# Masked scores stay in PSUM through exponential, copy and low pass

## The chip, the cores and the metric

The kernel runs on one core of a Trainium2 chip. The metric is the time of one execution on the device, in microseconds (us). Five engines work beside each other and are ordered by semaphores only: TensorE (PE in the profile; its weight loads are PEld), VectorE (DVE), ScalarE (ACT), GpSimd (POOL) and SyncE (SP), which issues most DMAs.

## The reference

Two layers in a row, in float32. First causal attention with a learned decay, for 8 batches of 8 heads, 576 positions and head size 64; then a two-layer network with a hard-swish product on the 4608 tokens.

```
scores = q @ k.T / 8
cum    = cumsum(log(clip(f, 1e-4, 1)))
scores = where(causal, -1e9, scores + cum[:, None] - cum[None, :])
attn   = exp(scores - max(scores)); attn = attn / (sum(attn) + 1e-9)
x      = (attn @ v), heads side by side      # 4608 x 512
h      = x @ w_in                            # 4608 x 2048
out    = (h * clip(h + 3, 0, 6) / 6) @ w_out # 4608 x 512
```

## The kernel before, in words

Precision is kept by splitting: a float32 operand becomes a high and a low float16 part, and a product takes three matmuls (high by high, high by low, low by high). The second part is made by a "low pass", x minus its high part.

The first batch is computed in another way (kinds A and B, lines 565 to 596), within the first 140 us or so, while the weights are loaded and split. The other 56 heads are of kind F and go through `rows` (line 621); this is what the change touches. A head is done in two halves, given by `NAT = ((1, 4, 0), (2, 3))`: each number c is a block of up to 128 query rows, with RB[c] + RR[c] keys before and in it (192, 576, 64 and 320, 448). For each half:

- L636 and L639: TensorE writes the scores of the blocks to one PSUM buffer `pn` of 1024 columns, which is two banks of 512. `PLACE` gives the column at which each block starts. The pool `ps_s` has two such buffers, so in effect one for each half.
- L647: VectorE adds the causal mask W, scales, and takes each row's extreme into `mc`. Its result goes to `pp`, a float32 tile in SBUF (832 columns, two buffers).
- L656: ScalarE takes the exponential, from `pp` to `pp`, with the row's extreme as bias.
- L673: ScalarE copies `pp`, scaled, as float16 into the tile `hl` (a `ring` buffer): the high part.
- L619, the helper `low`: VectorE computes the low part from `pp` and the high part, into `hl`. A head has seven of these: 128x128 and 128x512, then one over two strips of 64 columns and one of 64x64 in the first half; 128x256, 128x384 and again the two strips in the second. The view `pair` takes the two strips from `at[a]` and `at[b]` and needs them in rising order.
- L694: a DMA transposes `hl` into `pT`, from which the products with V are computed (L719 to L724).

Beside this, the network's tiles (`moe_tile`: L808 to L810, L816 to L821, then L863 to L873) are issued in small units between the steps of a head by a credit count. GpSimd prepares the split Q and K of the coming heads (L463 to L476). A planner at build time sets the order on each engine from the order of issue, the dependencies and its own estimates of durations; on the chip each engine goes through its list in order.

`decay` (line 173) reads the decay factors f at the start, takes their logarithm and the running sum. Its tiles fs and lf use the same SBUF buffers as `pp` (tag Pp). `xT` is the transposed input of the network's tiles, two buffers, and is written by DMA from L775 on.

Of the kernel before, what the change touches and what calls it, by code (L numbers as in the profile page):

```python
# [11 lines left out]
F32 = mybir.dt.float32  # L12
# [8 lines left out]
def kernel(  # L21
# [12 lines left out]
    NHEAD, D, S = qk.shape  # L34
# [5 lines left out]
    P = 128  # L40
# [14 lines left out]
    p2 = ctx.enter_context(tc.tile_pool(name="p2", bufs=2))  # L55
# [32 lines left out]
    W = cpool.tile([P, 4 * P + P], BF16, name="W")  # L88
# [59 lines left out]
    xT = [cpool.tile([P, NCC, TT // P, 2, P], F16, name=f"xT{i}") for i in range(2)]  # L148
# [24 lines left out]
    def decay():  # L173
        warm = p2.tile([1, 1], F32, tag="m1", name="warm")
        nc.vector.memset(warm, 1.0)
        nc.scalar.activation(warm, warm, AF.Ln)
        fs = p2.tile([NHEAD, S], F32, tag="Pp", name="fs")
        nc.sync.dma_start(fs, f)
        yield
        zf = p2.tile([NHEAD, S], F32, tag="PHL", name="zf")  # L180
        nc.vector.memset(zf, 0.0)
        nc.vector.tensor_scalar(fs, fs, 1e-4, 1.0, op0=ALU.max, op1=ALU.min)
        lf = p2.tile([NHEAD, S], F32, tag="Pp", name="lf")
        nc.scalar.activation(lf, fs, AF.Ln)
        nc.scalar.activation(warm, lf[0:1, 0:1], AF.Exp)
        cum = p2.tile([NHEAD, S], F32, tag="xf", name="cum", bufs=1)
        nc.vector.tensor_tensor_scan(cum[:, :], lf, zf, 0.0, op0=ALU.add, op1=ALU.add)
        nc.vector.tensor_scalar(cs[:, 0, :], cum, 8.0, None, op0=ALU.mult)
        d = nc.vector.scalar_tensor_tensor(
            cs[:, 1, :], cum, 8.0, cs[:, 0, :].bitcast(F32), op0=ALU.mult, op1=ALU.subtract  # L190
        )
        decayed.append(d.ins)
        yield
# [415 lines left out]
    o = 0  # L609
    for half in NAT:  # L610
        for c in half:
            HT[c] = o
            o += (2 * c + 1) * P
    PLACE = {1: 0, 4: 192, 0: 768, 3: 0, 2: 512}
    ringh = [t.bitcast(F16) for t in ring]
    clean = set()

    def low(out_, x, hi):
        nc.vector.scalar_tensor_tensor(out_, x, PSC, hi, op0=ALU.mult, op1=ALU.subtract)  # L619

    def rows(v):
        i, j = v % NQK, v % NL
        n = VH[v][1]
        pT = p2.tile([P, 3200], F16, tag="PHL", name=f"pT_{v}")
        mc = MF[v % 2]
        e0 = 0
        for half in range(2):
            pn = ps_s.tile([P, 1024], F32, tag="S", name=f"pn_{v}_{half}")
            hl = ringh[(2 * v + half) % NRING]
            for c in NAT[half]:  # L630
                o, r, kw = PLACE[c], RR[c], RB[c] + RR[c]
                cut = [0] + [x for x in (512 - o, ) if 0 < x < kw] + [kw]
                qs = slice(RB[c], RB[c] + r)
                for a, e in zip(cut, cut[1:]):
                    dst = pn[:r, o + a:o + e]
                    nc.tensor.matmul(  # L636
                        dst, TQ[i][0:D + 4, qs], TK[i][0:D + 4, a:e], start=True, stop=False
                    )
                    nc.tensor.matmul(  # L639
                        dst, T7[j][:, qs], T1[j][:, a:e], start=False, stop=True  # L640
                    )
            pp = p2.tile([P, 832], F32, tag="Pp", name=f"pp_{v}_{half}")
            at, w = {}, 0
            for x, c in enumerate(NAT[half]):
                o, r, kw = PLACE[c], RR[c], RB[c] + RR[c]
                at[c] = w
                nc.vector.tensor_tensor_reduce(  # L647
                    pp[:r, w:w + kw], pn[:r, o:o + kw], W[:r, 4 * P + r - kw:4 * P + r],
                    -0.125, 3.0e38, ALU.add, ALU.min, accum_out=mc[:r, e0 + x:e0 + x + 1],
                )  # L650
                w += kw
            e1 = e0 + len(NAT[half])
            for x, c in enumerate(NAT[half]):
                r, kw = RR[c], RB[c] + RR[c]
                x_ = pp[:r, at[c]:at[c] + kw]
                nc.scalar.activation(  # L656
                    x_, x_, AF.Exp, bias=mc[:r, e0 + x:e0 + x + 1], scale=-1.0
                )
            e0 = e1
            yield  # L660

            def pair(t, a, b):
                return t[:, a:a + 2 * (b - a)].rearrange("p (n w) -> p n w", n=2)[:, :, 0:64]

            h0 = {c: GH[half][c] + c * P + 64 for c in NAT[half]}
            slot = (2 * v + half) % NRING
            if 0 in NAT[half] and slot not in clean:
                nc.gpsimd.memset(hl[64:, h0[0] - 64:h0[0] + 64], 0.0)
                if w_out_done:
                    clean.add(slot)  # L670
            for c in NAT[half]:
                r, kw, a = RR[c], RB[c] + RR[c], GH[half][c]
                nc.scalar.activation(  # L673
                    hl[:r, h0[c]:h0[c] + kw], pp[:r, at[c]:at[c] + kw], AF.Copy, scale=PSC
                )
                if c:
                    low(
                        hl[:r, a:a + c * P], pp[:r, at[c] + 64:at[c] + kw],
                        hl[:r, h0[c] + 64:h0[c] + kw],
                    )  # L680
            a, b = NAT[half][:2]
            low(
                pair(hl, h0[a] - 64, h0[b] - 64), pair(pp, at[a], at[b]),
                pair(hl, h0[a], h0[b]),
            )
            if 0 in NAT[half]:
                low(
                    hl[:64, h0[0] - 64:h0[0]], pp[:64, at[0]:at[0] + 64],
                    hl[:64, h0[0]:h0[0] + 64],
                )  # L690

            w = sum((2 * c + 1) * P for c in NAT[half])
            d = HT[NAT[half][0]]
            nc.sync.dma_start_transpose(  # L694
                pT[:, d:d + w].rearrange("p (g t) -> p g t", t=P), hl[:, 0:w]
            )
            yield pT
# [213 lines left out]


    dec = decay()
    w_in_q = w_in_work()
    w_out_q = w_out_work()
# [93 lines left out]
    for i, (kind, n) in enumerate(VH):  # L1009
# [13 lines left out]
        if moved is not None:  # L1023
            done(moved)
            moved = None
        rates[0] = F_RATE[0] if kind == "B" else F_RATE[b] if b < 2 else even(h)
        sg = rows(i) if kind == "F" else scores(i)
        front = ahead and VH[i + 2][0] != "F"
        next(sg)
# [93 lines left out]
```

## Time and profile before

| | |
|---|---|
| median of 3 runs | 1063.89 us (1061.79 to 1065.01) |
| the profiled execution | 1063.62 us, span in the trace 1061.8 us |
| mean granted TensorE clock | 0.977 |
| TensorE busy | 1023.8 us, 96% |
| VectorE busy | 779.1 us, 73% |
| ScalarE busy | 600.5 us, 57% |
| GpSimd busy | 422.2 us, 40% |

The shares are means over the whole span. The profile divides it: where an engine is busy all the time and where it waits differs by stage, and a line of code stands in the profile as L and its number in the listing.

### The profile page before, as it was taken

What the parts mean: (1) busy time and instruction counts of PE and PEld (TensorE: products, weight loads), DVE (VectorE), ACT (ScalarE), POOL (GpSimd) and SP (SyncE); (2) the same over time, 40 slices, a digit from 0 to 9 for tenths busy, and PEclk for the clock granted to TensorE, in tenths of its full rate; (3) what the DMA queues carried; (4) which work ended last, traced back from release to release, by engine and by line L of the source; (5) the groups of instructions that cost most, each with busy time, mean ns of one, the idle gap of its engine ahead of it and who ended that gap; (6) DMA issues with size and microseconds to landing.
All of it is one profiled execution on the core that took longest, in us unless ns stands there. A gap on an engine that the chain in (4) does not pass through costs nothing.

```text
span 1061.8 us, 20746 instructions
## 1 busy us (share of the span) xinstructions
PE 1023.8 (96%) x7833; PEld 616.2 (58%) x7833; DVE 779.1 (73%) x1927; ACT 600.5 (57%) x1190; POOL 422.2 (40%) x430
## 2 busy tenths in 40 slices
PE   6789999889999999999999999999999999999998
PEld 4567867655555755555555755555555755545545
DVE  8788998999986679876976679876976788505500
ACT  4678676776664557655654556655754577405500
POOL 7455774565452444444334244444424442000000
PEclk8699999889999999999999999999999999999999
DMA  8665325778555555466443474456444534410000
GB/s 301 212 193 161 92 59 125 148 139 169 115 94 101 117 142 104 80 131 149 83 88 89 101 157 97 97 127 143 82 94 84 103 80 78 81 30 11 1 20 30
DMA packets 248415, 114.34 MB, mean 108 GB/s; under 512 B 224788, under 2 KB 226124, under 8 KB 248316
## 3 DMA queue, kind: packets, MB, share of 16 engines
q1 hardware_dynamic: 248284, 113.03, 46.9%
q8 instruction: 61, 1.00, 0.4%
q14 instruction: 38, 0.31, 0.1%
q10 hardware_dynamic: 32, 0.01, 0.0%
HBM read 47.93 MB, written 9.73 MB: 54 GB/s over the span
## 4 chain that ended last, share of the span: by engine, by line
PE 66%; DVE 19%; DMA 6%; ACT 4%; issue 3%; SPq 1%; DVEq 0%; ACTq 0%
PE po L863 11%; PE po L865 11%; PE po L864 11%; PE ph L808 6%; PE ph L810 6%; PE ph L809 6%; DVE ring L619 6%; DMA vst<-in_vS_dram 3%; PE pn L639 3%; PE pn L636 3%; DVE pp L647 2%; DVE gT L821 2%; DVE r L819 2%; DVE vm L382 1%; DVE w L311 1%
## 5 line engine op out<-in xcount | busy, mean ns | idle before, releaser
L619 DVE SCALAR_TENSOR_TENSOR ring<-pp,ring 128x128 f16<-128x128 f32 x392 | 237.4, 645 | 51.1 <-ACT ring L673 49.0
L463 POOL TENSOR_SCALAR TK<-ST 64x576 fp32r<-64x576 f32 (+1 forms) x68 | 57.2, 841 | 430.2 <-PE pn L636 395.0
L863 PE MATMUL po<-w,gT 128*128 128x512 f16 x560 | 210.1, 382 | 0.0
L864 PE MATMUL po<-w,gT 128*128 128x512 f16 x560 | 209.2, 381 | 0.5 <-DVE w L311 0.3
L865 PE MATMUL po<-w,gT 128*128 128x512 f16 x560 | 209.1, 381 | 0.0
L808 PE MATMUL ph<-xT,w 128*128 128x512 f16 (+1 forms) x576 | 201.7, 359 | 6.2 <-DVE r L819 6.2
L809 PE MATMUL ph<-xT,w 128*128 128x512 f16 (+1 forms) x576 | 201.0, 358 | 0.0
L810 PE MATMUL ph<-xT,w 128*128 128x512 f16 (+1 forms) x576 | 200.9, 358 | 0.0
L656 ACT ACTIVATE pp<-pp,MF 128x192 f32<-128x192 f32 x280 | 147.7, 554 | 89.8 <-DVE MF L647 88.7
L647 DVE CUSTOM_DVE_ANT_0 pp<-pn,W 128x192 f32<-128x192 f32 x280 | 123.3, 480 | 20.2 <-PE pn L639 19.9
L636 PE MATMUL pn<-TK,TQ 68*128 68x192 f32 x336 | 125.3, 386 | 3.4 <-DVE MF L647 3.0
L820 ACT CAST gT<-r 128x512 f16<-128x512 f32 (+1 forms) x144 | 81.4, 567 | 76.7 <-DVE r L819 75.8
L816 ACT ACTIVATE r<-ph,bias_r,SC 128x512 f32<-128x512 f32 (+1 forms) x144 | 103.2, 721 | 35.6 <-PE ph L810 23.7
L673 ACT ACTIVATE ring<-pp 128x192 f16<-128x192 f32 x280 | 119.6, 458 | 1.5
L821 DVE TENSOR_TENSOR gT<-r,gT 128x512 f16<-128x512 f32 (+1 forms) x144 | 101.2, 706 | 23.9 <-ACT gT L820 22.4
L819 DVE SCALAR_TENSOR_TENSOR r<-r,ph 128x512 f32<-128x512 f32 (+1 forms) x144 | 88.7, 618 | 40.0 <-ACT r L816 40.0
L639 PE MATMUL pn<-T,T 128*128 128x192 f32 x336 | 115.4, 369 | 0.0
L476 POOL TENSOR_TENSOR T<-ST,T 64x576 fp32r<-64x576 f32 (+1 forms) x68 | 108.3, 1593 | 5.1
L473 POOL TENSOR_TENSOR T<-ST,TQ 64x576 fp32r<-64x576 f32 (+2 forms) x68 | 96.4, 1417 | 5.4
L873 ACT ACTIVATE o<-po,SC 128x512 f32<-128x512 f32 (+1 forms) x37 | 24.8, 669 | 123.6 <-PE po L865 122.2
L865 PEld LDWEIGHTS <-gT 128*128 128x128 f16 x560 | 54.7, 98 | 68.3 <-issue 8.8
L864 PEld LDWEIGHTS <-gT 128*128 128x128 f16 x560 | 54.8, 98 | 59.8 <-issue 5.4
(150 smaller groups left out, 2010.6 us busy)
## 6 DMA issues: line engine op xcount, KB each, us to landing
ST<-in_qk_dram SPq DMA_DIRECT2D x64, 288.0 KB
out_dram<-o SPq DMA_DIRECT2D x33, 256.0 KB
ring<-in_w_out_dram SPq DMA_DIRECT2D x16, 512.0 KB
vst<-in_vS_dram SPq DMA_DIRECT2D x7, 1040.0 KB
ring<-in_w_in_dram SPq DMA_DIRECT2D x9, 512.0 KB
w<-in_w_in_dram SPq DMA_DIRECT2D x7, 512.0 KB
vst<-in_vS_dram SPq DMA_DIRECT2D x14, 130.0 KB
pT<-ring SPq DMA_TRANSPOSE x112
```

The costliest lines, as they stand in the source:

```text
L619: nc.vector.scalar_tensor_tensor(out_, x, PSC, hi, op0=ALU.mult, op1=ALU.subtract)
L636: nc.tensor.matmul(dst, TQ[i][0:D + 4, qs], TK[i][0:D + 4, a:e], start=True, stop=False)
L639: nc.tensor.matmul(dst, T7[j][:, qs], T1[j][:, a:e], start=False, stop=True)
L647: nc.vector.tensor_tensor_reduce(pp[:r, w:w + kw], pn[:r, o:o + kw], W[:r, 4 * P + r - kw:4 * P + r], -0.125, 3.0e38, ALU.add, ALU.min, ac ...
L656: nc.scalar.activation(x_, x_, AF.Exp, bias=mc[:r, e0 + x:e0 + x + 1], scale=-1.0)
L808: nc.tensor.matmul(ph, w1[0][:, cc, fs_], xh, start=(cc == 0), stop=False)
L809: nc.tensor.matmul(ph, w1[0][:, cc, fs_], xl, start=False, stop=False)
L810: d = nc.tensor.matmul(ph, w1[1][:, cc, fs_], xh, start=False, stop=(cc == NCC - 1))
L821: nc.vector.tensor_tensor(gT[:, 1, fc, c0:c1], r, gT[:, 0, fc, c0:c1], op=ALU.subtract)
L863: nc.tensor.matmul(po, g[:, 0, fc, ts_], w2[:, fc, 0, c], start=(fc == 0), stop=False)
L864: nc.tensor.matmul(po, g[:, 0, fc, ts_], w2[:, fc, 1, c], start=False, stop=False)
L865: d = nc.tensor.matmul(po, g[:, 1, fc, ts_], w2[:, fc, 0, c], start=False, stop=(fc == NFC - 1))
```

## The change

`pp` is no longer a tile of its own: the masked scores go back to where they were read, in the PSUM buffer `pn`; the exponential is taken there, and the copy and the low pass read from there. `PLACE` exchanges the places of c = 2 and c = 3, so that `pair` finds the two strips in rising order. fs and lf, which used the buffers of `pp`, lie in the first `xT` buffer.

```
-        fs = p2.tile([NHEAD, S], F32, tag="Pp", name="fs")
+        fs = xT[0].bitcast(F32).rearrange("p a c l t -> p (a c l t)")[0:NHEAD, 0:S]
...
-        lf = p2.tile([NHEAD, S], F32, tag="Pp", name="lf")
+        lf = xT[0].bitcast(F32).rearrange("p a c l t -> p (a c l t)")[0:NHEAD, S:2 * S]
...
-    PLACE = {1: 0, 4: 192, 0: 768, 3: 0, 2: 512}
+    PLACE = {1: 0, 4: 192, 0: 768, 2: 0, 3: 512}
...
-            pp = p2.tile([P, 832], F32, tag="Pp", name=f"pp_{v}_{half}")
-            at, w = {}, 0
+            pp, at = pn, PLACE
             for x, c in enumerate(NAT[half]):
                 o, r, kw = PLACE[c], RR[c], RB[c] + RR[c]
-                at[c] = w
                 nc.vector.tensor_tensor_reduce(
-                    pp[:r, w:w + kw], pn[:r, o:o + kw], W[:r, 4 * P + r - kw:4 * P + r],
+                    pn[:r, o:o + kw], pn[:r, o:o + kw], W[:r, 4 * P + r - kw:4 * P + r],
                     -0.125, 3.0e38, ALU.add, ALU.min, accum_out=mc[:r, e0 + x:e0 + x + 1],
                 )
-                w += kw
```

## Rows read from the trace of the kernel before

**Rows 1.** The page's busy time of TensorE, us, share of the span, instructions.

```profile
PE 1023.8 (96%) x7833; PEld 616.2 (58%) x7833; DVE 779.1 (73%) x1927; ACT 600.5 (57%) x1190; POOL 422.2 (40%) x430
```

**Rows 2.** Windows: length, busy PE, PEld, DVE, ACT, POOL; granted clock, DMA.

```profile
140.00:200.00 60.00, 53.86 (x459) 37.97 (x458) 55.08 (x155) 40.15 (x89) 33.06 (x29) 0.98 0.59 123
200.00:300.00 100.00, 95.92 (x794) 58.56 (x795) 95.27 (x247) 68.76 (x146) 54.24 (x51) 0.94 0.68 135
300.00:400.00 100.00, 100.00 (x875) 60.44 (x873) 70.67 (x181) 52.70 (x108) 42.66 (x42) 1.00 0.55 115
...
930.00:1000.00 70.00, 70.00 (x464) 37.38 (x462) 22.75 (x33) 26.42 (x40) 0.00 (x0) 1.00 0.04 13
```

**Rows 3.** Waits of TensorE, 140 to 300 us: us in total, times, longest.

```profile
PE pav L719 <- DMA pT<-ring: 4.3, 3, 1.7
PE pn L636 <- DVE MF L647: 3.0, 1, 3.0
PE ph L808 <- DVE r L819: 2.0, 2, 1.2
```

**Rows 4.** Waits of TensorE, 300 to 930 us (all of them).

```profile
PE ph L808 <- DVE r L819: 2.2, 6, 0.7
```

**Rows 5.** The page's costliest groups: count, busy us, mean ns, idle before.

```profile
L619 DVE SCALAR_TENSOR_TENSOR ring<-pp,ring 128x128 f16<-128x128 f32 x392 | 237.4, 645 | 51.1 <-ACT ring L673 49.0
...
L647 DVE CUSTOM_DVE_ANT_0 pp<-pn,W 128x192 f32<-128x192 f32 x280 | 123.3, 480 | 20.2 <-PE pn L639 19.9
```

**Rows 6.** Groups by line and form, 896 to 930 us.

```profile
L619 DVE SCALAR_TENSOR_TENSOR ring<-pp,ring 128x128 f16<-128x128 f32 x6 | 1.7, 283 | 0.1
...
L619 DVE SCALAR_TENSOR_TENSOR ring<-pp,ring 128x512 f16<-128x512 f32 x2 | 1.4, 690 | 1.2 <-ACT ring L673 1.2
...
L619 DVE SCALAR_TENSOR_TENSOR ring<-pp,ring 128x384 f16<-128x384 f32 x2 | 1.1, 548 | 0.0
...
L619 DVE SCALAR_TENSOR_TENSOR ring<-pp,ring 128x256 f16<-128x256 f32 x2 | 0.8, 414 | 0.0
...
L619 DVE SCALAR_TENSOR_TENSOR ring<-pp,ring 64x64 f16<-64x64 f32 x2 | 0.4, 212 | 0.0
```

**Rows 7.** Timeline, 208 to 226 us: start us, duration us, what, [idle before].

```profile
208.99 0.39 PE L636 MATMUL pn<-TK,TQ 68*128 68x320 f32 x1
...
214.09 3.19 DVE L619 SCALAR_TENSOR_TENSOR ring<-pp,ring 128x256 f16<-128x256 f32 x3
...
215.19 1.47 POOL L476 TENSOR_TENSOR T<-ST,T 64x576 fp32r<-64x576 f32 x1
...
218.22 0.61 DVE L647 CUSTOM_DVE_ANT_0 pp<-pn,W 128x448 f32<-128x448 f32 x1
...
218.89 0.64 PE L636 MATMUL pn<-TK,TQ 68*128 68x320 f32 x1 [2.99 <-DVE MF L647]
...
223.26 2.10 DVE L619 SCALAR_TENSOR_TENSOR ring<-pp,ring 128x384 f16<-128x384 f32 x2
```

**Rows 8.** Line 819's instructions: durations in ns, least, median, most.

```profile
L819 DVE SCALAR_TENSOR_TENSOR r<-r,ph x144: 373/674/690, 98.3 to 1006.6; 128x512 f32<-128x512 f32 x112, 128x256 f32<-128x256 f32 x32
```

**Rows 9.** Groups of VectorE by line, 150 to 250 us, the costliest.

```profile
L619 DVE SCALAR_TENSOR_TENSOR ring<-pp,ring 128x128 f16<-128x128 f32 (+4 forms) x67 | 38.8, 619 | 0.1
```

**Rows 10.** Groups by line and form, whole span: ScalarE's exponentials of 576 columns.

```profile
L656 ACT ACTIVATE pp<-pp,MF 128x576 f32<-128x576 f32 x56 | 42.7, 762 | 2.5 <-DVE MF L647 2.4
...
L593 ACT ACTIVATE pf<-ps,bias_p 128x576 f32<-128x576 f32 x8 | 5.9, 736 | 0.0
```

**Rows 11.** Line 775's transposing DMAs into x: durations, first and last start.

```profile
L775 SPq DMA_TRANSPOSE xT<-xhl x36: 1190/1233/3077, 58.6 to 927.7; - x36
```

**Rows 12.** Timeline, 320 to 337 us: scores and the last lows of one half.

```profile
320.87 0.44 PE L636 MATMUL pn<-TK,TQ 68*128 68x192 f32 x1
...
326.81 1.02 DVE L619 SCALAR_TENSOR_TENSOR ring<-pp,ring 128x512 f16<-128x512 f32 x3 [1.19 <-ACT ring L673]
...
336.90 0.44 PE L636 MATMUL pn<-TK,TQ 68*128 68x192 f32 x1
```

## The prediction

> **What bounds the kernel now.** I read the busy table first: TensorE is busy 96% of the span [rows 1]. A busy figure this high says little about how near an engine is to its peak, so the next view is busy time by stretch [rows 2]. In it the reader should see three stages. From 300 us on TensorE has no gap at the full granted clock (1.00) while VectorE has 29 us of slack in a hundred; in the last stage GpSimd is idle and VectorE busy for a third. Nothing that VectorE saves there can shorten anything. From 140 to 300 us it is otherwise: TensorE is idle for 60.00 - 53.86 = 6.1 us and 100.00 - 95.92 = 4.1 us, together 10.2 us, while VectorE is busy for 55.08 of 60 and 95.27 of 100 us. That stage alone is bound by VectorE. It also shows granted clocks of 0.98 and 0.94, which is 0.02 x 60 + 0.06 x 100 = 7.2 us of full-speed clock not given, next to the idle time.
>
> The view of waits says who was late there [rows 3]. The largest wait is for a transposed P: that DMA starts when the last low pass of its half is written. The next is for the masks of a scores buffer, the third for the eviction of an MoE tile. All end on VectorE or on a DMA that VectorE released. After 300 us the same view has 2.2 us in all [rows 4]. So the most that a lighter VectorE can give back is 10.2 + 7.2 + 2.2 = 19.6 us, a little less since clock lost in idle time is counted twice. Everything before 140 us stays as it is: the change touches nothing there except two buffers.
>
> **The change: the low pass.** The low pass (L619) is the costliest VectorE group, and the edit to it is the one that carries the gain. Its rows look wrong for their size: 392 instructions at a mean of 645 ns [rows 5], although the window in which GpSimd has no work left shows the same forms at 690, 548, 414, 283 and 212 ns [rows 6]. A head has one each of the first three, three of 128x128 and one of 64x64: 690 + 548 + 414 + 3 x 283 + 212 = 2713 ns. The 392 are 56 heads, so undisturbed they would take 56 x 2.71 = 152 us, and they take 392 x 0.645 = 253 us. Some 101 us are lost beside GpSimd. The timeline shows it happening: three lows that should take 0.41 + 0.55 + 0.28 us take 3.19 us from 214.09 on, beside a GpSimd subtraction that starts at 215.19; the masks of the same stretch come behind them and end at 218.83, and TensorE, idle for 2.99 us, starts its scores at 218.89 [rows 7].
>
> What would an instruction of this kind take with one input in PSUM and one in SBUF? The MoE product (L819) is the same operation with exactly that pair of inputs: over 144 instructions in all stages its maximum is 690 ns for a median of 674 [rows 8], so it is never stretched, and 128x512 costs what the undisturbed low pass costs [rows 6]. I take the low pass after the change at its undisturbed figures. That is 101 us less on VectorE over the kernel. In the stretch that matters, 150 to 250 us, it is 67 x 619 = 41.5 us [rows 9] against 67/7 x 2.71 = 26.0 us, so 15.5 us less. Bounds: nothing, if the stretching had another cause; 15.5 us, if all goes.
>
> The Trainium skill says otherwise on one point: "Perfetto Trace Analysis", section "Optimizing Scalar/DVE Operations", gives VectorE about 60 ns of access overhead on SBUF and 125 ns on PSUM. Its 65 ns on 67 lows would leave about 11 us of the 15.5, and, with half of 19.6 x 11/15.5, a forecast some 3 us later than mine. The rows show no such difference at 128x512 (at most 690 ns with an input in PSUM, 690 without), so the sum goes by them.
>
> **The masks and ScalarE.** The mask pass (L647, 123.3 us in 280 instructions, [rows 5]) now writes PSUM where it reads. No row of before shows VectorE reading and writing one bank. From below it costs nothing (same count, same columns); from above, if a read and a write in one bank halved its rate, it doubles: 123 us more, which would eat the low pass's 101 us. I take nothing, because the low pass and the MoE product move the same columns at the same rate whether or not an operand is in PSUM. The exponentials now read and write PSUM: the one exponential that reads PSUM takes 736 ns at 576 columns, the SBUF one 762 [rows 10]. So ScalarE gains up to 26 ns on each of 560 instructions, 15 us, or nothing. It is not the bound in any row of [rows 2]; I count zero, and what would uncover it is ScalarE being held by VectorE (second rival).
>
> **Buffers at nothing.** fs and lf go into the first x buffer. They are read in the opening of the kernel and the first transposed x lands only from 58.6 us on [rows 11], so no wait arises; instruction counts are the same. The new PLACE changes banks, not the number or order of matmuls.
>
> **The wait that is added.** A scores buffer is now held from its first matmul to its last low pass; before, to its last mask. There are two, one for each half. In the later stage this is covered: scores begin at 320.87, the last low ends at 326.81 + 1.02 = 327.83, the next scores for that buffer begin at 336.90 [rows 12]. The hold is 7.0 us and 9.1 us are to spare. Between 150 and 250 us it is not: scores that begin at 208.99 have their last low at 223.26 + 2.10 = 225.36, a hold of 16.4 us, and the next ones began at 218.89, 6.5 us before that [rows 7]. Left in the same order TensorE would wait these 6.5 us instead of 2.99. Behind the waiting scores stand MoE and P.V matmuls, since TensorE goes in order; whoever evicts those waits in turn. Against it stand the lows: of the 16.4 us, 3.19 - 1.24 = 1.95 us are stretch in the lows ahead of its masks and about 1.3 us more (2.10 against 0.548 + 0.283) in its last ones. And the order is not fixed: the planner that sets it sees the longer hold, and can put MoE matmuls ahead of the scores.
>
> **Sum.** The reachable 19.6 us are reduced by the new hold. With VectorE down from 96 in a hundred toward 80 in the stretch, its backlog should go, and with it the three waits of [rows 3]; the hold keeps some. Between all and nothing I take half: 9.8 us. The profiled execution took 1063.62 us (span 1061.8 and 1.8 around it), which lies 0.3 us under the median of the runs, 1063.89. So 1063.6 - 9.8 = 1053.8, say 1054 us. The later 900 us stay as they are.
>
> **Rivals.**
> No gain: the idle time between 140 and 300 us belongs to the order and to transposes, not to VectorE's speed, or the in-place masks eat what the lows give. For it: the largest wait of [rows 3] names a DMA. Against it: that DMA follows a low pass. Time: 1060.4 to 1066.8, most likely the old 1063.6.
>
> Slower, by the hold: between 150 and 250 us, 67/7 = 9.6 heads pass, one in 10.4 us [rows 9]. A hold over 10.4 us cannot keep this pace with one buffer for each half, and that is the point from which it decides. Midway between the two holds seen (7.0 and 16.4) is 11.7 us: 9.6 x (11.7 - 10.4) = 12.5 us, all on TensorE, nothing regained: 1076 us. For it: the 16.4 us. Against it: VectorE's lighter load, and MoE matmuls to put between.
>
> Slower, by shared banks: the copy (ScalarE) and the low pass (VectorE) now read the same bank. If two engines cannot be in one bank at a time, then in the half with c = 1, 4, 0, whose c = 4 lies across both banks, copy and low must alternate: the copy of c = 4 waits for the low of c = 1 (0.28 us), that of c = 0 for the low of c = 4 (0.69 us), about 1.0 us of held ScalarE in every head. Behind it on ScalarE stand the evictions of the MoE tiles, for which TensorE waits. Over the 46 heads outside the stretch that is 46 us if nothing hides it; the 2.2 us of [rows 4] say that eviction has slack, so a third, 15 us, which with the gain kept gives 1069 us. The Trainium skill states the rule behind it: "PSUM — Partial Sum Buffer", section "PSUM bank collisions raise a hardware error", says that two engines in one bank and quadrant collide, reads included, and have to be ordered. No row of before shows the two engines in one bank.
>
> **How the numbers follow.** Forecast (1043 to 1060): 0.57. No gain: 0.20. Hold: 0.14. Banks: 0.09. Faster by over 0.3% (3.2 us, about what the three runs can tell from no change) is the first, 0.57; within 0.3% the second, 0.20; slower the last two, 0.23. The low end is the reachable sum, 1063.6 - 19.6 = 1044, less 1 us for the spread of the runs. The high end takes in the banks' 1069 and the lighter part of the hold, 1072; above it lies some 0.08.
>
> **What would show it.** Right: L619 at 2.7 us for a head with no stretched instruction; VectorE's busy time down by some 85 to 100 us; TensorE's idle time from 140 to 300 us below 6 us at a clock of 0.97 or more; nothing changed after 930 us but its start. Wrong: scores matmuls (L636) that wait for the low pass by more than 10 us in total, which is the hold; ScalarE's copies (L673, now with almost no idle time before them) waiting for lows by 40 us or more together with longer MoE waits, which is the banks; L647 well over 480 ns in the mean, which is the in-place mask. If all three are absent and the time is still 1064, the idle time was the order's.

## The result and the profile after

The changed kernel takes 1076.03 us (1075.33 to 1077.67), before 1063.89: a ratio of 1.0119, 95% interval 1.0099 to 1.0138. It is slower by 1.2%; the forecast was 1054 us, a gain. The profiled execution after took 1077.67 us, span 1075.9. Line numbers fall by two to three: masks L647 is now L645, exponentials L656 L653, copies L673 L670, V products L719 L716, the network's L808 to L810 and L863 to L865 now L805 to L807 and L860 to L862.

The busy table of after answers to [rows 1]. VectorE and GpSimd are lighter, TensorE is busy for longer.

```profile
PE 1029.8 (96%) x7833; PEld 625.7 (58%) x7833; DVE 699.6 (65%) x1927; ACT 586.3 (54%) x1190; POOL 395.5 (37%) x430
```

The costliest groups of after, for those of [rows 5], with the exponentials and the copies beside them (busy us, mean ns, idle before and what ended it):

```profile
L653 ACT ACTIVATE pn<-pn,MF 128x192 f32<-128x192 f32 (+1 forms) x280 | 132.8, 496 | 132.1 <-DVE MF L645 110.1
...
L645 DVE CUSTOM_DVE_ANT_0 pn<-pn,W 128x192 f32<-128x192 f32 x280 | 134.8, 501 | 75.6 <-PE pn L639 72.7
L619 DVE SCALAR_TENSOR_TENSOR ring<-pn,ring 128x128 f16<-128x128 f32 (+1 forms) x392 | 137.0, 386 | 58.1 <-ACT ring L670 56.7
L670 ACT ACTIVATE ring<-pn 128x192 f16<-128x192 f32 (+1 forms) x280 | 114.2, 433 | 39.6 <-DVE ring L619 36.5
```

The low pass did what was forecast: 386 ns in the mean against 645, 100 us less. The in-place mask pays 21 ns. New is the 36.5 us in which ScalarE's copies wait for lows. VectorE's busy time falls by 79.5 us, from 779.1 to 699.6. So no operation became dear enough to explain the loss, which must lie in waits. Two windows of after, for those of [rows 2] (length, busy PE, PEld, DVE, ACT, POOL, granted clock, DMA share, GB/s):

```profile
200.00:300.00 100.00, 85.83 (x710) 54.66 (x707) 70.86 (x223) 59.34 (x132) 45.15 (x48) 0.88 0.57 118
...
930.00:1000.00 70.00, 70.00 (x482) 36.64 (x482) 21.42 (x41) 24.26 (x40) 0.00 (x0) 1.00 0.14 35
```

VectorE is no longer full between 200 and 300 us (70.86 against 95.27), and yet TensorE is idle there for 14.2 us instead of 4.1, at a clock of 0.88 instead of 0.94. Cut at other places, the same view separates two stretches. First after:

```profile
140.00:230.00 90.00, 84.02 (x701) 57.96 (x700) 68.14 (x213) 53.59 (x121) 34.62 (x36) 0.98 0.47 101
230.00:280.00 50.00, 35.83 (x286) 24.09 (x284) 33.06 (x103) 25.60 (x57) 23.41 (x27) 0.76 0.64 130
...
330.00:930.00 600.00, 597.39 (x4778) 345.93 (x4776) 407.11 (x1142) 340.03 (x691) 227.01 (x238) 1.00 0.52 107
```

and before:

```profile
140.00:230.00 90.00, 80.61 (x703) 57.64 (x703) 83.89 (x235) 60.74 (x137) 52.08 (x47) 0.92 0.61 126
230.00:280.00 50.00, 49.16 (x420) 28.42 (x419) 48.31 (x126) 33.27 (x67) 26.44 (x24) 1.00 0.79 162
...
330.00:930.00 600.00, 597.80 (x4804) 343.12 (x4803) 460.20 (x1125) 346.73 (x683) 232.59 (x229) 1.00 0.49 105
```

Up to 230 us TensorE does better after the change: 3.4 us less idle time, and 0.06 x 90 = 5.4 us of clock more. From 230 to 280 us it loses 49.16 - 35.83 = 13.3 us and 0.24 x 50 = 12 us of clock (the two overlap, since a clock that is low in idle time costs nothing). From 330 to 930 us the difference is 0.4 us. So the loss shows in one stretch of 50 us.

What TensorE did up to 230 us shows why. In groups by line of 140 to 230 us, before, and the masks of that stretch (five to a head):

```profile
L863 PE MATMUL po<-w,gT 128*128 128x512 f16 x41 | 16.4, 405 | 0.0
...
L647 DVE CUSTOM_DVE_ANT_0 pp<-pn,W x39: 207/477/753, 139.9 to 227.8; 128x576 f32<-128x576 f32 x8, 64x64 f32<-64x64 f32 x8, 128x320 f32<-128x320 f32 x8, 128x448 f32<-128x448 f32 x8
```

The same two groups after:

```profile
L860 PE MATMUL po<-w,gT 128*128 128x512 f16 x61 | 23.2, 380 | 0.8 <-DVE r L816 0.8
...
L645 DVE CUSTOM_DVE_ANT_0 pn<-pn,W x30: 215/500/767, 140.7 to 225.3; 128x192 f32<-128x192 f32 x6, 128x576 f32<-128x576 f32 x6, 128x320 f32<-128x320 f32 x6, 64x64 f32<-64x64 f32 x6
```

The network's line L860 has issued 61 matmuls instead of 41 (L861 and L862 likewise), and six heads are masked instead of eight. The planner, which sees the longer hold, filled TensorE with the network's first tile. That looks like a gain, and is work taken from later: from 230 to 280 us the same group has 4 matmuls where there were 23 before. What is then left is the chain of heads, and the timeline of after shows its pace (start us, duration us, what, [idle before]; rows of three engines, put together):

```profile
234.66 0.44 PE L636 MATMUL pn<-TK,TQ 68*128 68x192 f32 x1
235.90 0.37 DVE L645 CUSTOM_DVE_ANT_0 pn<-pn,W 128x192 f32<-128x192 f32 x1 [4.76 <-PE pn L639]
237.68 0.66 DVE L645 CUSTOM_DVE_ANT_0 pn<-pn,W 128x448 f32<-128x448 f32 x1
237.92 1.74 ACT L653 ACTIVATE pn<-pn,MF 128x192 f32<-128x192 f32 x4 [4.77 <-DVE MF L645]
...
242.99 2.10 DVE L619 SCALAR_TENSOR_TENSOR ring<-pn,ring 128x256 f16<-128x256 f32 x6
243.44 0.81 ACT L670 ACTIVATE ring<-pn 128x448 f16<-128x448 f32 x2 [1.07 <-DVE ring L619]
...
239.02 0.19 PE L721 MATMUL pav<-v,pT 128*128 128x65 f16 x1
244.87 0.50 PE L636 MATMUL pn<-TK,TQ 68*128 68x192 f32 x1 [5.67 <-ACT ring L670]
...
253.56 0.33 PE L636 MATMUL pn<-TK,TQ 68*128 68x192 f32 x1 [0.87 <-ACT v L413]
260.21 0.24 PE L716 MATMUL pav<-v,pT 128*128 128x65 f16 x1 [4.76 <-DMA pT<-ring]
...
263.00 0.50 PE L636 MATMUL pn<-TK,TQ 68*128 68x192 f32 x1 [0.44 <-issue]
270.93 0.62 PE L805 MATMUL ph<-xT,w 128*128 128x512 f16 x1
```

The engines take turns: masks to 238.3, exponentials from 237.9, copies and lows to 245.1. The next scores start at 244.87, behind the copies and lows that read their buffer (the row x6 holds the lows of both halves; the view names a copy); before, the buffer would have been free with the masks. From 239.2 to 244.87 TensorE has nothing it may do. The heads follow 10.2, 8.7 and 9.4 us apart. Only the first of these starts ends a wait for the buffer; ahead of the last, TensorE waited 4.76 us for a transposed P. The two largest waits of TensorE from 140 to 300 us (total, times, longest), for [rows 3]:

```profile
PE pav L716 <- DMA pT<-ring: 8.5, 3, 4.8
PE pn L636 <- ACT ring L670: 5.7, 1, 5.7
```

The largest is again a transposed P, which follows the last low; the second is the hold itself. Other waits on L636 add only 1.3 us.

What TensorE lacks in the gap is x. One DMA moves the x of a pair of heads, and the network's tile of a batch needs four pairs. Here are the second and the fourth of the second batch, before:

```profile
212.52 1.99 SPq L775 DMA_TRANSPOSE xT<-xhl  x1
...
252.89 1.34 SPq L775 DMA_TRANSPOSE xT<-xhl  x1
```

and after:

```profile
223.20 1.42 SPq L772 DMA_TRANSPOSE xT<-xhl  x1
...
266.43 1.72 SPq L772 DMA_TRANSPOSE xT<-xhl  x1
```

The fourth starts 13.5 us later, and the span is longer by 14.1 us. Of that delay 10.7 us are there at the second pair already, in the stretch in which TensorE looks better. Before, TensorE begins the network's second tile at 253.6 us. After, it begins it at 232.3 with the x that is there, nine matmuls of each line, and goes on at 270.93, behind the fourth pair:

```profile
L805 PE MATMUL ph<-xT,w x9: 379/379/650, 232.3 to 250.6; 128*128 128x512 f16 x9
```

### The profile page after: what moved, and what is told of

Same layout as the page of the kernel before. It is cut to its first block, busy times and chain, and to the rows that moved or that the text cites. A ratio compares the mean times of both kernels' runs of the same rounds, so it can differ in the third digit from the quotient of the medians.

```text
span 1075.9 us, 20862 instructions
## 1 busy us (share of the span) xinstructions
PE 1029.8 (96%) x7833; PEld 625.7 (58%) x7833; DVE 699.6 (65%) x1927; ACT 586.3 (54%) x1190; POOL 395.5 (37%) x430
## 4 chain that ended last, share of the span: by engine, by line
PE 82%; DVE 8%; DMA 5%; ACT 2%; issue 1%; SPq 1%; DVEq 0%; ACTq 0%
PE po L860 11%; PE po L862 11%; PE po L861 11%; PE ph L805 10%; PE ph L806 10%; PE ph L807 9%; PE pn L636 4%; PE pn L639 4%; DMA pT<-ring 2%; PE pav L720 2%; PE pav L721 2%; PE pav L719 1%; PE pav L727 1%; DMA ring<-in_w_in_dram 1%; DMA vst<-in_vS_dram 1%
## 5 line engine op out<-in xcount | busy, mean ns | idle before, releaser
L463 POOL TENSOR_SCALAR TK<-ST 64x576 fp32r<-64x576 f32 (+1 forms) x68 | 50.6, 744 | 473.2 <-PE pn L636 433.1
L860 PE MATMUL po<-w,gT 128*128 128x512 f16 x560 | 208.7, 380 | 0.8 <-DVE r L816 0.8
L861 PE MATMUL po<-w,gT 128*128 128x512 f16 x560 | 208.3, 379 | 0.0
L862 PE MATMUL po<-w,gT 128*128 128x512 f16 x560 | 208.1, 379 | 0.0
L805 PE MATMUL ph<-xT,w 128*128 128x512 f16 (+1 forms) x576 | 202.1, 360 | 5.7 <-DVE r L816 5.7
L653 ACT ACTIVATE pn<-pn,MF 128x192 f32<-128x192 f32 (+1 forms) x280 | 132.8, 496 | 132.1 <-DVE MF L645 110.1
L807 PE MATMUL ph<-xT,w 128*128 128x512 f16 (+1 forms) x576 | 200.9, 360 | 0.0
L645 DVE CUSTOM_DVE_ANT_0 pn<-pn,W 128x192 f32<-128x192 f32 x280 | 134.8, 501 | 75.6 <-PE pn L639 72.7
L619 DVE SCALAR_TENSOR_TENSOR ring<-pn,ring 128x128 f16<-128x128 f32 (+1 forms) x392 | 137.0, 386 | 58.1 <-ACT ring L670 56.7
L670 ACT ACTIVATE ring<-pn 128x192 f16<-128x192 f32 (+1 forms) x280 | 114.2, 433 | 39.6 <-DVE ring L619 36.5
L636 PE MATMUL pn<-TK,TQ 68*128 68x192 f32 x336 | 114.5, 363 | 7.0 <-ACT ring L670 5.7
L476 POOL TENSOR_TENSOR T<-ST,T 64x576 fp32r<-64x576 f32 (+1 forms) x68 | 101.6, 1494 | 5.1
L639 PE MATMUL pn<-T,T 128*128 128x192 f32 x336 | 101.9, 330 | 0.0
L473 POOL TENSOR_TENSOR T<-ST,TQ 64x576 fp32r<-64x576 f32 (+2 forms) x68 | 92.1, 1355 | 5.4
L862 PEld LDWEIGHTS <-gT 128*128 128x128 f16 x560 | 54.7, 98 | 63.9 <-issue 3.4
L861 PEld LDWEIGHTS <-gT 128*128 128x128 f16 x560 | 54.6, 98 | 61.4 <-issue 4.5
L806 PEld LDWEIGHTS <-w 128*128 128x128 f16 x576 | 56.8, 99 | 55.7 <-issue 10.2
```

The costliest lines, as they stand in the source:

```text
L636: nc.tensor.matmul(dst, TQ[i][0:D + 4, qs], TK[i][0:D + 4, a:e], start=True, stop=False)
L639: nc.tensor.matmul(dst, T7[j][:, qs], T1[j][:, a:e], start=False, stop=True)
L645: nc.vector.tensor_tensor_reduce(pn[:r, o:o + kw], pn[:r, o:o + kw], W[:r, 4 * P + r - kw:4 * P + r], -0.125, 3.0e38, ALU.add, ALU.min, ac ...
L653: nc.scalar.activation(x_, x_, AF.Exp, bias=mc[:r, e0 + x:e0 + x + 1], scale=-1.0)
L670: nc.scalar.activation(hl[:r, h0[c]:h0[c] + kw], pp[:r, at[c]:at[c] + kw], AF.Copy, scale=PSC)
L805: nc.tensor.matmul(ph, w1[0][:, cc, fs_], xh, start=(cc == 0), stop=False)
```

## The experiments

Times are medians, ratios stand to the kernel before on the same chip.

**Parts that should cost nothing.** The kernel before with the new places of fs and lf and the new PLACE; the scores still go to SBUF.

```
+        fs = xT[0].bitcast(F32).rearrange("p a c l t -> p (a c l t)")[0:NHEAD, 0:S]
+        lf = xT[0].bitcast(F32).rearrange("p a c l t -> p (a c l t)")[0:NHEAD, S:2 * S]
+    PLACE = {1: 0, 4: 192, 0: 768, 2: 0, 3: 512}
```

> The kernel before with two parts of the change alone: fs and lf in the first x buffer, and the new PLACE; the masked scores go to SBUF as before. Hold theory (the loss comes from the scores buffer being held to the last low pass): as before, 1061 to 1067 us. Rival (the other bank order or the moved buffers disturb the order that the planner makes): 1070 us or more.

1063.95 us, 1.0009 (0.9985 to 1.0033). They cost nothing; the loss is in the PSUM part.

**The relief without a hold.** The kernel before, with GpSimd's two subtractions left out for the 56 heads. It leaves out the low parts of Q and K, so the scores lack a correction; the matmuls on them still run.

```
         nc.gpsimd.tensor_scalar(T1[j][D:, 0:nk], s[D:, 0:nk], **one)
+        if VH[v][0] == "F":
+            return
...
+        nc.gpsimd.memset(T7[i].bitcast(F32)[D:, 2 * QA:], 0.0)
```

> The kernel before, with GpSimd's two subtractions of each head of kind F left out (the low parts of q and k, so the scores lose a correction): the relief of the low passes without any hold. If relief was worth what the prediction took, 1050 to 1058 us with the low passes at a mean below 0.5 us; if the idle time of TensorE between 140 and 300 us belongs to the order or to other waits, 1061 to 1067 us.

1050.0 us, 0.9873 (0.9841 to 0.9905). In its groups the low pass, with all its inputs in SBUF, is shorter, 435 ns in the mean, though not yet the 2713 / 7 = 388 of undisturbed ones. That group, and the window:

```profile
L621 DVE SCALAR_TENSOR_TENSOR ring<-pp,ring 128x128 f16<-128x128 f32 x392 | 155.3, 435 | 55.4 <-ACT ring L675 53.3
...
230.00:280.00 50.00, 50.00 (x421) 28.49 (x417) 44.36 (x121) 35.72 (x73) 12.38 (x16) 1.00 0.74 147
```

So the relief is worth some 14 us where nothing is held: more than the 9.8 that the forecast took. (GpSimd is relieved here as well, and its part in the 14 us is not separated.)

**The hold without anything else.** The kernel before, with a small VectorE instruction behind the lows of each half that reads `pn` once more; the scores still go to SBUF.

```
+            kept = p2.tile([P, 2], F32, tag="kept", name=f"kept_{v}_{half}")
+            nc.vector.tensor_tensor(
+                kept, pn.rearrange("p (a b) -> p a b", a=2)[:, :, 0],
+                hl[:, h0[NAT[half][0]] - 64:h0[NAT[half][0]] - 62], op=ALU.add,
+            )
```

> The kernel before with the hold alone: everything goes through SBUF as before, but a two-column VectorE addition after the low passes of each half reads the scores buffer, so that it comes free only then (112 instructions of about 0.15 us more on VectorE, 17 us). Hold theory: lows are still stretched beside GpSimd, so the hold is longer than in the changed kernel, TensorE lacks work near 250 us for longer, and the time is over 1076, some 1085 to 1100 us. Rival (the loss comes from sharing banks or from masks written in place): 1062 to 1068 us.

1070.27 us, 1.0069 (1.0045 to 1.0092): the hold costs, but some 7 us, less than expected. The 112 added instructions are in this too: 148 ns each, 16.5 us of VectorE over the kernel. Up to 280 us its windows show the same pattern as after's, weaker:

```profile
140.00:230.00 90.00, 83.79 (x742) 58.33 (x740) 78.18 (x244) 58.10 (x130) 40.70 (x41) 1.00 0.58 117
...
230.00:280.00 50.00, 43.24 (x363) 24.67 (x360) 46.02 (x124) 33.94 (x71) 26.34 (x26) 0.97 0.72 132
```

The better row up to 230 us comes here without a lighter low pass (its mean is 629 ns). So in the profile after, too, that row by itself is no sign of the relief; the new order gives it too. The network's first tile is put ahead here as well, with 58 matmuls by 230 us where there were 41 before:

```profile
L868 PE MATMUL po<-w,gT 128*128 128x512 f16 x58 | 21.7, 379 | 0.9 <-DVE r L824 0.9
```

So a hold by itself goes with that order. But the fourth pair's x is not late here:

```profile
249.47 1.23 SPq L780 DMA_TRANSPOSE xT<-xhl  x1
```

And about half of the added idle time of TensorE lies behind 280 us: 3.8 us instead of none from 280 to 330, and 5.0 instead of 2.2 from 330 to 930. This run shows that a hold costs, not that after loses by it in the same way.

**Where the loss is.** The change in the first ten of the 56 heads alone; for the other 46 alone the condition is `n < H + 10`.

```
             pp, at = pn, PLACE
+            if n >= H + 10:
+                pp = p2.tile([P, 832], F32, tag="Pp", name=f"pp_{v}_{half}")
+                at, w = {}, 0
+                for c in NAT[half]:
+                    at[c] = w
+                    w += RB[c] + RR[c]
```

> The changed kernel in the first ten heads of kind F alone; the other 46 go through SBUF as before. Hold theory: the whole loss is made in the first ten heads, so 1073 to 1079 us. Rival (ScalarE and VectorE alternating in every head costs something everywhere): at most half of the loss, 1064 to 1070 us.

> The reverse: the first ten heads of kind F through SBUF, the other 46 in PSUM. Hold theory: TensorE is never without network tiles after 300 us, so the longer hold costs nothing there: 1060 to 1066 us. Rival (alternation costs in every head): 1069 us or more.

First ten alone: 1081.94 us, 1.0178 (1.0134 to 1.0222). The other 46: 1065.04 us, 1.0007 (0.9984 to 1.003). All the loss comes from the first ten, where the fourth pair's x is late again (270.01); the 46 gain nothing from the change, as the forecast held of this stage. The window of the first kernel, and then of the second:

```profile
230.00:280.00 50.00, 35.62 (x302) 23.52 (x298) 31.99 (x101) 26.91 (x62) 25.55 (x27) 0.76 0.57 121
```

```profile
230.00:280.00 50.00, 48.59 (x415) 27.90 (x412) 45.19 (x125) 33.69 (x68) 24.07 (x24) 1.00 0.72 157
```

Why ten heads alone lose more than all 56 is not settled; each edit also gives the planner other dependencies and so another order.

**Which half.** The change in the second half of each head alone (blocks 2 and 3, one bank each), and in the first half alone (blocks 1, 4, 0, where 4 lies across both banks). The edit is the one above under `if half == 0:` and `if half == 1:`.

> The changed kernel for the second half of each head alone (blocks 2 and 3, one bank each); the first half goes through SBUF as before. If the hold alone decides, one of two buffers is held long and the loss is about half, 1066 to 1072 us. If the sharing of banks by block 4, which lies across both, lengthens the chain, there is little loss here, 1062 to 1067 us, and more in the next kernel.

> The changed kernel for the first half of each head alone (blocks 1, 4 and 0; block 4 lies across both banks); the second half goes through SBUF as before. If the hold alone decides, as the kernel with the second half, 1066 to 1072 us. If bank sharing by block 4 lengthens the chain, most of the loss is here, 1071 us or more.

Second half alone: 1064.9 us, 1.0000 (0.9973 to 1.0027). First half alone: 1074.3 us, 1.0104 (1.0070 to 1.0138), with this window:

```profile
230.00:280.00 50.00, 42.09 (x329) 25.52 (x329) 40.39 (x100) 30.12 (x61) 24.88 (x26) 0.86 0.54 112
```

The first half carries nearly the whole loss. Is that its hold, or the sharing of banks? The hold alone in the first half, with the data in SBUF (the edit of the hold run under `if half == 0:`):

> The kernel before with the hold alone in the first half of each head (a two-column VectorE addition after its low passes that reads the scores buffer); all data stay in SBUF. If the hold as such makes the loss of the kernel that has the first half in PSUM (ratio 1.010), this one is at 1070 us or more; if bank sharing by block 4 makes it, 1062 to 1067 us.

1067.6 us, 1.0030 (1.0009 to 1.0052), with 56 added instructions. Of the 1.04% in the first half a hold by itself makes some 0.3; the other 0.7 comes with the data being in PSUM. Whether that is the sharing of banks, the masks and exponentials there, or another planned order, these runs do not tell apart.

**Copies ahead of lows.** The changed kernel, with all copies of a half issued ahead of its lows, so that ScalarE and VectorE do not alternate there.

```
                     hl[:r, h0[c]:h0[c] + kw], pp[:r, at[c]:at[c] + kw], AF.Copy, scale=PSC
                 )
+            for c in NAT[half]:
+                r, kw, a = RR[c], RB[c] + RR[c], GH[half][c]
                 if c:
```

> The changed kernel with all copies of a half issued before its low passes, so that ScalarE need not wait for a low pass to leave a bank. If ScalarE's waits for low passes (36.5 us in 57 waits after the change) are what lengthens the chain, most of the loss goes: 1062 to 1069 us. If the loss is the hold as such, or the bank order of masks and exponentials, the time stays at 1071 to 1080 us.

1071.4 us, 1.0069 (1.0049 to 1.0089). The copies' idle time goes from 39.6 to 2.5 us:

```profile
L670 ACT ACTIVATE ring<-pn 128x192 f16<-128x192 f32 (+1 forms) x280 | 101.4, 434 | 2.5 <-DMA pT<-ring 0.7
```

Some 0.5 of the 1.2% come back, and the time lies in the range put down for the other causes, 1071 to 1080 us. ScalarE's waits of this kind in after, over the whole span:

```profile
ACT ring L670 <- DVE ring L619: 36.5, 57, 3.0
```

and from 140 to 300 us:

```profile
ACT ring L670 <- DVE ring L619: 2.7, 5, 1.1
```

Only 2.7 of the 36.5 us lie in the stretch that loses. The alternation of copies and lows can thus be a part of the cause at most; and since this edit changes the planned order too, it is not shown that the 0.5% are owed to it.

**Exponentials out of PSUM.** The changed kernel, with the exponential written to SBUF; copies and lows read there, so the buffer is held to the last exponential only.

```
-                x_ = pp[:r, at[c]:at[c] + kw]
+                o, r, kw = PLACE[c], RR[c], RB[c] + RR[c]
+                at[c] = w
                 nc.scalar.activation(
-                    x_, x_, AF.Exp, bias=mc[:r, e0 + x:e0 + x + 1], scale=-1.0
+                    pp[:r, w:w + kw], pn[:r, o:o + kw], AF.Exp,
+                    bias=mc[:r, e0 + x:e0 + x + 1], scale=-1.0
                 )
+                w += kw
```

> The changed kernel with the exponential written to an SBUF tile: the masks are still written in place in PSUM, but the scores buffer comes free after the exponentials, and copy and low pass read SBUF as before the change. Hold theory: near the kernel before, 1061 to 1067 us, with the low passes stretched again to a mean of about 0.64 us. Rival (the masks in place in PSUM, whose accumulator read takes 0.14 us instead of 0.08, are the loss): 1073 us or more.

1070.9 us (1064.9 to 1078.2), 1.0074 (1.0038 to 1.0110). It lies between the theories and tells little. Its runs spread widely, and the profiled one is the fastest of them, so its trace is not read for the loss.

**The relief by another way.** If a low pass beside GpSimd waits for an instruction there to end, shorter instructions help without a hold. The kernel before, with each of GpSimd's subtractions cut in two, and in four.

```
-        nc.gpsimd.tensor_tensor(
-            T1[j][0:D, 0:nk], s[D:, 0:nk], T1[j][D:, 0:nk].bitcast(F32), op=ALU.subtract
-        )
+        for a in range(0, nk, nk // 2):
+            e = a + nk // 2
+            nc.gpsimd.tensor_tensor(
+                T1[j][0:D, a:e], s[D:, a:e], T1[j][D:, a:e].bitcast(F32), op=ALU.subtract
+            )
```

> The kernel before, with each of GpSimd's subtractions cut into two instructions of half the columns and nothing else changed. A stretched low pass never takes longer than its own time plus about one such subtraction, so if it waits for the one instruction that is under way, half-size ones should halve the stretch (some 50 us less on VectorE) without any hold: 1053 to 1061 us. If the low pass waits for GpSimd to have nothing queued, or GpSimd's own time grows too much, 1062 to 1068 us.

> The same with four instructions of a quarter of the columns each. If the stretch follows the length of one instruction it falls again, to about a quarter, 1050 to 1060 us; if the fixed cost of GpSimd's instructions takes it back, as the kernel with halves or slower.

In two: 1054.45 us, 0.9918 (0.9894 to 0.9942). In four: 1055.52 us, 0.9918 (0.9896 to 0.9940). Both beat both kernels; nothing more is won from two to four. In groups of the first:

```profile
L475 POOL TENSOR_TENSOR T<-ST,TQ 64x288 fp32r<-64x288 f32 (+2 forms) x136 | 124.2, 914 | 387.9 <-PE pn L643 352.7
L623 DVE SCALAR_TENSOR_TENSOR ring<-pp,ring 128x128 f16<-128x128 f32 x392 | 222.6, 608 | 51.4 <-ACT ring L677 49.6
```

The low pass's mean falls only from 645 to 608 ns, 15 us of VectorE where 50 were expected, and yet 9 us are won. The granted clock from 140 to 230 us is 0.98 in this run instead of 0.92, which is 5.4 us of the nine, and the fourth pair's x comes at 244.93, 8.0 us earlier than before. In quarters the mean falls further, and the time does not:

```profile
L623 DVE SCALAR_TENSOR_TENSOR ring<-pp,ring 128x128 f16<-128x128 f32 x392 | 202.1, 556 | 52.8 <-ACT ring L677 51.1
```

So the gain does not follow the stretch of the lows alone, and its cause is not shown.

## Why the prediction was wrong, step by step

**The low pass: right.** One input in PSUM was taken to end the stretching: 2.7 us for a head, against 7 x 0.386 = 2.70. Line 619 of after by source (least, median, most ns):

```profile
L619 DVE SCALAR_TENSOR_TENSOR ring<-pn,ring x392: 201/291/693, 154.4 to 935.4; 128x128 f16<-128x128 f32 x81, 64x64 f16<-64x64 f32 x29, 128x256 f16<-128x256 f32 x29, 128x384 f16<-128x384 f32 x29
```

No instruction is over 693 ns, beside GpSimd or not, and the input in PSUM brought no time of its own: 128x512 took 686 ns in the mean, against 690 undisturbed before. The Trainium skill, "SBUF — State Buffer", section "Who interferes with whom", says that a VectorE instruction with two SBUF inputs contends with a GpSimd instruction that reads SBUF, and that one with at most one, outside the 2-port modes, does not. This trace agrees: 645 ns in the mean with two, 386 with one.

**What the relief is worth: right in kind, small in size.** The forecast took 9.8 of 19.6 us; without GpSimd's subtractions 14 us came back. The rival "no gain" is wrong: with lighter low passes and no hold the time falls, by 14 us here and by 9 with the subtractions in two. How much of either is VectorE's alone is open.

**Masks in place: small, not nothing. Buffers: right.** The mask cost was taken as nothing; it is 134.8 - 123.3 = 11.5 us of VectorE, and 31.2 - 17.6 = 13.6 for 224 of the 280 reads of the accumulator behind them (last section). That is far from the upper bound of 123 and covered by the 100. Buffers cost nothing in their own run.

**The wait that is added: the step that failed.** The forecast weighed the 16.4 us hold and answered that the planner can put network matmuls ahead of the scores. It did just that, and there the reasoning broke. Matmuls put ahead are a stock, not a supply: the first tile was used up by 232 us, and the next one needs x, which is made by the very heads that they were put ahead of. The last po matmul of the tile in after, by source:

```profile
L862 PE MATMUL po<-w,gT x64: 377/379/392, 147.1 to 232.0; 128*128 128x512 f16 x64
```

and before:

```profile
L865 PE MATMUL po<-w,gT x64: 377/379/634, 146.7 to 253.4; 128*128 128x512 f16 x64
```

It ends 21 us earlier, the batch's last x comes 13.5 us later (266.43 against 252.89), and TensorE starves in the gap: 14.2 us idle from 230 to 280, at a clock of 0.76. Of the 19.6 us that might be regained, the forecast let the hold take back no more than half; the change lost 12 us instead. The rival "hold" named its point (one head in 10.4 us) and its time of 1076 us, which is what came. It had 0.14. That the number fits is in part luck. The rival reckoned 1.3 us for each of 9.6 heads and nothing regained; near the gap the heads follow at 8.7 to 10.2 us, inside its 10.4. And a hold alone makes 0.69%, not all of it in this stretch.

**Shared banks: wrongly placed, and not settled.** Copies wait 36.5 us for lows, 36.5 / 56 = 0.65 us for a head, near the 1.0 put down. Most of it is in the first half, as put down: 16.8 us stand before the copy of 64 columns alone, which shares a bank with block 4 but no data.

```profile
L670 ACT ACTIVATE ring<-pn 64x64 f16<-64x64 f32 x56 | 11.9, 213 | 17.2 <-DVE ring L619 16.8
```

But the price was sought in the 46 later heads, in the eviction of network tiles, and there it is nothing: 330 to 930 us is unchanged. The loss is in the first ten heads, where few of these waits are seen (2.7 us). That turns between the engines lengthen the chain of heads there is argued, not shown. The rule drawn on there, "PSUM — Partial Sum Buffer" of the Trainium skill, section "PSUM bank collisions raise a hardware error", says that the accesses have to be ordered. The trace agrees: before, the same copy waited 0.0 us.

**The signs.** Of the signs of being right, the lows came as said, and after 930 us TensorE is busy throughout, as before. VectorE's busy time fell by 79.5 us, short of the 85 to 100; the masks and the reads behind them take a part back. The idle time of TensorE from 140 to 300 us was to be below 6 us at a clock of 0.97 or more, and is 20.2 us at 0.91: this sign told. The signs of being wrong did not. "Scores that wait for the low pass by more than 10 us" did not come (5.7 us on L636): the largest wait stands on the V products instead (8.5 us). The copies' waits stayed under their 40 us, and the masks' mean rose only to 501 ns.

**Open.** The place of the loss is shown, each by its own run: the PSUM part, the first ten heads, and of each head the first half. What delays the heads there is not. The hold (0.69%) and what copies first give back (0.5%) add up to the 1.19% on paper. But the relief, 1.3% by itself, should stand against them, the hold alone does not make the second batch's x late, and with the copies first 0.69% of loss are still there. So something more is lost. With the hold ended at the exponentials, and copies and lows in SBUF again, the median is still 0.74% up; the taking of turns of masks and exponentials may be it, but those runs spread widely and no run separates it. Nor does any run hold the planner's order fixed, so a worse order by itself remains a rival.

## What to carry to other kernels

A buffer that is released later is free while the waiting engine has other work, and that other work is a stock: ask when it runs out and whether the held chain is what refills it. A hold is to be set against the pace of the tightest stage, not of the mean. Idle time can be the late sign of a delay made earlier: look at when the chain delivers. Where two engines contend, look first for a cure without a hold: instructions of half the columns on the other engine gave 0.8% here, though for reasons not fully traced.

## What the runs showed of the hardware that was not expected

Reading the accumulator costs more when the main result goes to PSUM: first before, then after, groups by form.

```profile
L647 DVE DVE_READ_ACCUMULATOR2_ANT MF<- 128x1 f32 x224 | 17.6, 79 | 0.0
```

```profile
L653 ACT ACTIVATE pn<-pn,MF 128x576 f32<-128x576 f32 x56 | 40.1, 716 | 1.3
...
L645 DVE DVE_READ_ACCUMULATOR2_ANT MF<- 128x1 f32 x224 | 31.2, 139 | 0.0
```

It is 139 ns instead of 79, more than the mask pass itself pays. Where half of each head is masked in PSUM, the mean lies between, at 109 and 110 ns. ScalarE, on the other hand, is faster from PSUM to PSUM: 716 ns for 576 columns, against 762 from SBUF to SBUF and 736 from PSUM to SBUF [rows 10]. The clock fell with the idle time: in this 10-us window of after it is 0.50, the lower level of 1.2 GHz, behind the gap from 255.5 to 260.2 us; from 244 to 250 us, behind the gap at 239, it is 0.50 too.

```profile
260.00:270.00 10.00, 6.92 (x75) 6.18 (x76) 6.50 (x21) 5.05 (x12) 4.79 (x6) 0.50 0.70 142
```
